# Four layers on one core: an instruction order planned with other delays, single score rounds, sorted waits, and the last layer's output weights multiplied into its key-value sum

## The chip, the core and the metric

The kernel runs on one core of a Trainium2 chip. Its engines work side by side: TensorE (PE; its weight loads stand as PEld), VectorE (DVE), ScalarE (ACT), GpSimd (POOL) and SyncE (SP, here the issuer of all DMAs). The metric is the device time of one execution in microseconds; lower is better. The profile is that of one further execution of the same program.

## The reference

The input x is 2048 rows of 512 columns, in bfloat16. Four layers follow each other, each with a layer norm in front and a residual addition behind. Layers 0 and 2 (called A, same weights) are softmax attention with 32 query heads of size 16 that share one key and one value head. Layers 1 and 3 (called B, same weights) are linear attention with 32 heads.

```python
def _A_ref(x, wq, wk, wv, wo):
    q = (x @ wq).reshape(B, S, H, Dh).transpose(0, 2, 1, 3)
    k, v = x @ wk, x @ wv
    scores = einsum("bhqd,bkd->bhqk", q, k) * (Dh ** -0.5)
    o = einsum("bhqk,bkd->bhqd", softmax(scores), v)
    return o.transpose(0, 2, 1, 3).reshape(B, S, H * Dh) @ wo

def _B_ref(x, wqkv, wo):
    q, k, v = ...
    phi = lambda t: where(t > 0, t + 1, exp(t)) + 1e-6
    pq, pk = phi(q), phi(k)
    kv = einsum("bhsd,bhse->bhde", pk, v)
    z = einsum("bhsd->bhd", pk)
    num = einsum("bhqd,bhde->bhqe", pq, kv)
    den = einsum("bhqd,bhd->bhq", pq, z)[..., None] + 1e-6
    return (num / den).transpose(0, 2, 1, 3).reshape(B, S, D) @ wo

x = x + _A_ref(_layernorm(x), A_wq, A_wk, A_wv, A_wo)
x = x + _B_ref(_layernorm(x), B_wqkv, B_wo)
x = x + _A_ref(_layernorm(x), A_wq, A_wk, A_wv, A_wo)
x = x + _B_ref(_layernorm(x), B_wqkv, B_wo)
```

## The kernel before

**The planner.** The program is not written in its final order. A `Planner` runs a small event simulation while the kernel is built: each operation is created with the engines it may run on, a planned duration, a latency `lat` until its result counts as there, a priority (lower goes first), and the buffers it reads and writes. Python generators (`process`) create operations as flags, buffers (`acq`) and finished operations allow. When an engine is free, `_dispatch1` gives it the ready operation of the lowest priority number, and that order is what is written out, engine by engine. `emit` puts the semaphore waits in front of each instruction: of all operations it depends on, the latest one of each engine, and skips what that engine has waited for already. Each engine then works through its list strictly in order, so an instruction whose input is late holds up all that stand behind it. The planned durations stand as constants (`QK_DUR`, `PV_DUR`, `QK_LAT`, `SWITCH` for a change of the way TensorE's array is divided) or in the calls.

**Layers 0 and 2** (`run_a`). The 2048 rows are 16 tiles of 128. Scores are made in blocks of 128 keys by 512 columns (four heads of a query tile; `j` is one of four row strips of TensorE's array); each layer has 2048 blocks. A score round (L807) issues up to four blocks, one for each row strip. ACT takes two or three blocks of a round at once and writes exponentials (`PT`, L973), out of two sets of three PSUM banks. DVE takes single blocks: it turns a score into the bits of a bfloat16 power of two by one addition and maximum (`FB`, L1049), and after four such blocks makes three shifted copies (L1080), so that each of these blocks is used four times with four weights. A DVE block rides in a round with ACT's blocks, either in the spare bank 7 (`dve_open`, allowed while DVE has under `BLO` us of work queued) or in the third bank of a set (`dve_split`, limits `BLS` and `BLT`). Blocks for DVE are allowed only once the layer's last key tile is there (`KGATE`). The exponentials are multiplied by the values into PSUM bank 6 (L861), four column strips abreast, and DVE collects each segment (L1103, L1105). While TensorE would idle, small matmuls without use are inserted (L906, in other phases L793). Each finished query tile is normalised (L1122 to L1133) and multiplied by `wo` (`epilogue`), and becomes the input of layer 1 or 3.

**Layers 1 and 3** (`run_b`). `tile_` norms a tile and makes its keys and values (`pk`, `va`); `q_` makes its queries: 16 matmuls (L732), then `phi`, which is one Exp on ACT (L1205) and two operations on DVE (L1206, L1208). All this runs, tile by tile, between the exponentials of the layer before. `kv_` sums keys times values over the tiles (L1308), with a column of ones in `va` that gives the key sum; for the last tile it masks the sums into block-diagonal weights `zb` (128x8 a group, L1332) and `kvz` (128x128 a group, L1336). Then, for each tile: `den` multiplies the queries by `zb` (L1358, L1360) and DVE takes reciprocals (L1364); `main` multiplies the queries by `kvz` (L1416), DVE multiplies by the reciprocals (`OB`, L1420), TensorE transposes (L1435), ACT or DVE copies (`OTB`, L569), TensorE multiplies by the output weights `wo2` (L575) and DVE adds the result to x (L1448). In layer 3 a store to DRAM (SP) follows each tile.

The one activation table that the program loads is at its start (L562), with a small Exp.

Of the kernel before, what the change touches and what calls it, by code (L numbers as in the profile page):

```python
# [7 lines left out]
FP32 = mybir.dt.float32  # L8
# [27 lines left out]
class Planner:  # L36
# [3 lines left out]
    def __init__(self, nc):  # L40
        self.nc = nc
        self.now = 0.0
        self.events = []
        self.seq = 0
        self.ready = {e: [] for e in ENGS}
        self.busy = {e: False for e in ENGS}
        self.until = {e: 0.0 for e in ENGS}
        self.order = {e: [] for e in ENGS}
        self.writer = {}
        self.readers = {}  # L50
        self.flags = {}
# [5 lines left out]
        self.port = 0.0  # L57

# [63 lines left out]
    def _dispatch(self, e):  # L122
        self._dispatch1(e)
        if e == PE and not self.busy[e] and self.idle:
            self.due = [t for t in self.due if t > self.now]
            for f in self.idle:
                f()

    def _dispatch1(self, e):
        if self.busy[e]:  # L130
            return
        h = self.ready[e]
        held = []
        while h:
            x = heapq.heappop(h)
            o = x[2]
            if o.eng is not None:
                continue
            dur, fn = o.opts[e]
            if o.port and self.port > self.now:  # L140
                held.append(x)
                continue
            if e == PE and STICK and o.mode != "row" and o.mode != self.mode != "row":
                like = [y for y in h if y[2].eng is None and y[2].mode == self.mode and y[0] <= o.prio + STICK]
                if like:
# [12 lines left out]
            o.eng, o.fn = e, fn  # L158
            self.order[e].append(o)
            self.busy[e] = True  # L160
            self.until[e] = self.now + dur
            if o.cols:
                self.work(o.cols)
            if o.begun:
                self.at(self.now, o.begun)
            self.at(self.now + dur, lambda: self._freed(e, o))
# [4 lines left out]
        if held and not self.busy[e] and e != PE:  # L171
            self.at(self.port, lambda: self._dispatch(e))
# [123 lines left out]
    def emit(self, e, eng):  # L296
        waited = {}
        for o in self.order[e]:
            need = {}
            for d in o.deps:  # L300
                if not d.isdma and d.eng == e and e not in (DV, AC, PO):
                    continue
                k = ("dma", d.slot) if d.isdma else d.eng
                if k not in need or need[k].value < d.value:
                    need[k] = d
            for k, d in need.items():
                if waited.get(k, 0) >= d.value:
                    continue
                waited[k] = d.value
                eng.wait_ge(d.sem, d.value)  # L310
            ins = o.fn(eng)
            if o.sem is not None:
                ins.then_inc(o.sem, 16 if o.isdma else 1)


class Seg:
# [11 lines left out]
    def take(self, js, back=False):  # L328
# [31 lines left out]
BLO = 3.0  # L360
BLT = 4.0
# [6 lines left out]
DENS = {1: [[0], [1], [2], [3], [4], [5], [6], [7], [8, 9], [10, 11], [12, 13], [14, 15]],  # L368
        3: [[0], [1, 2], [3, 4, 5], [6, 7, 8, 9], [10, 11, 12], [13, 14, 15]]}
# [3 lines left out]
RESA = {1: (), 3: ()}  # L373
# [18 lines left out]
def bass_interleave_layers__grouped_kv_mqa__linear_attn_block__prompt_kernel(  # L392
# [42 lines left out]
    eps1 = sb("eps1", [1, H], BF16)  # L435
    warm = sb("warm", [P, 1], FP32)
# [117 lines left out]
    pool_op(lambda e: e.memset(eps1[:], 1e-6), ["eps"], dur=0.1, prio=2.1)  # L554
    pool_op(lambda e: e.memset(mask8[:], 1.0), ["mask8"], dur=0.3, prio=2.3)
# [242 lines left out]
    def run_a(L):  # L798
# [34 lines left out]
        def pv_try():  # L833
# [32 lines left out]
            o = op({PE: (PV_DUR, fn)}, reads=list({x[3] for x in items}) + [("V" if x[5] is None else "VW", x[0]) for x in items], writes=[B_(ACC)], prio=2.0, lat=0.13, mode="col")  # L866
# [46 lines left out]
        def act_stream():  # L913
# [4 lines left out]
            state["on"] = lin["a"] = True  # L918
            while True:
# [53 lines left out]
                ex = op({AC: (0.05 + 0.4267 * n, lambda e, n=n, s_=s_, p_=p_: e.activation(PT[:, p_, 0:n * 512], ps[:, s_ * 512:(s_ + n) * 512], ACTF.Exp, scale=EXPSC, bias=EXPBIAS))},  # L973
                        writes=bk + [("PT", p_)], prio=1.0, lat=0.17)
                ex.begun = lambda n=n: pl.due.append(pl.now + 0.05 + 0.4267 * n + 0.17)
                pl.give_after(sets, s_, [ex] if split is None else [ex, p1])
                pv_post(ex, [(sg, kt, j, PT[:, p_, i * 512:(i + 1) * 512], ("PT", p_)) for i, (sg, kt, j) in enumerate(group)], [n, [], pt_pool, p_])
            state["done"] = True
            pv_kick()
# [64 lines left out]
        def dve_take(extra, own):  # L1044
# [4 lines left out]
            o = op({DV: (0.60, lambda e: e.tensor_scalar(out=dst.bitcast(I16), in0=bank(b), scalar1=VB, scalar2=VLO, op0=ALU.add, op1=ALU.max))},  # L1049
# [7 lines left out]
            return o  # L1057

# [7 lines left out]
        def dve_shifts(blk, f_, hold):  # L1066
# [3 lines left out]
            for w in range(1, NSH):  # L1070
# [8 lines left out]
                en, du = (PO, n / 1165.0 + 0.25) if pool else (DV, n / 3840.0 + 0.066)  # L1079
# [117 lines left out]
    ph_pool = Pool_(range(NPH))  # L1197

    def run_b(L):
# [3 lines left out]
        def phi(b, dst, key, pr, n=D, join=None, after=()):  # L1203
            i = yield ("acq", ph_pool, pr)
            op({AC: (0.07 + n / 1200.0, lambda e: e.activation(phE[:, i, 0:n], bank(b, n), ACTF.Exp))}, reads=[B_(b)], writes=[("phE", i)], prio=min(pr, 0.9))  # L1205
# [22 lines left out]
        def crit_v(t, sl, pr):  # L1228
# [5 lines left out]
            for h in range(2):  # L1234
                src, dst = bank(bs[h], 256).rearrange("p (h d) -> p h d", d=DH), va_v[:, sl, 16 * h:16 * h + 16, 0:DH]
                c = op({AC: (AH_DUR, lambda e, dst=dst, src=src: e.copy(dst, src))}, writes=[B_(bs[h]), ("va", sl)], prio=pr, join=l)
                l = l or c
                pl.give_after(banks, bs[h], [c])
            yield ("ops", pl.ws(("va", sl)))

        def tile_(t):
# [19 lines left out]
            src, dst = bank(b).rearrange("p (h d) -> p h d", d=DH), va_v[:, sl, :, 0:DH]  # L1261
            if t >= CRIT:
# [7 lines left out]
        def q_(t):  # L1270
            pr = base(t) + 0.01 * t + 0.2
            yield ("flag", ("xnT", L, t))
            yield from until(("xnT", t))
            b = yield ("acq", banks, pr)
            mm4(bank(b), lambda g, k: wqkv[:, k, g * P:(g + 1) * P], lambda k: xnT[:, k, t * P:(t + 1) * P], [("xnT", t), "wqkv"], b, pr)
            yield from phi(b, QT[:, t, :], ("QT", t), pr)
            pl.flag(("bq", L, t))

# [175 lines left out]
        for t in range(T):  # L1454
            pl.process(tile_(t))
            pl.process(q_(t))
            pl.process(main(t))
        for ts in DENS[L]:
            pl.process(den(ts))
        for gi, ts in enumerate(KVG):  # L1460
            pl.process(kv_(gi, ts))
# [50 lines left out]
```

## Time and profile before

| what | us |
|---|---|
| median of 3 runs (1555.47, 1555.51, 1560.37) | 1555.51 |
| the profiled execution | 1556.79 |
| its span, first to last instruction | 1555.1 |
| granted TensorE clock, mean over the span | 0.996 |
| first exponential on ACT starts | 13.6 |
| last exponential of layer 0 ends, first of layer 2 starts | 736.2, 759.5 |
| last exponential of layer 2 ends | 1508.0 |
| first denominator of layer 3 starts | 1519.1 |
| last addition of layer 3 ends | 1552.7 |

The times from the third row on are counted from the span's first instruction. Busy times are unions: where two instructions of an engine overlap, the stretch counts once, while the mean of a group is that of single instructions. A line of the groups gives the kernel line, engine, operation, output and inputs with their shapes, the count, busy us and mean ns, then the idle time in front and what ended most of it. A line of the waits says who waited for whom: us in total, times, longest.

### The profile page before, as it was taken

Reading aid. Unit: us, or ns where it says so; the run is one execution under the profiler, and the core shown is the slowest. Engines: PE = TensorE matmul, PEld = TensorE weight load, DVE = VectorE, ACT = ScalarE, POOL = GpSimd, SP = SyncE. Lnnn points to the kernel's source line nnn. Section 1 sums busy time; section 2 is a strip of 40 time slices with the busy share of each in tenths; the row PEclk is TensorE's granted clock in tenths of the full one; section 3 lists DMA queues with packets and bytes.
Section 4 is the critical chain, followed back from the end, with each engine's and each line's share of the span. In section 5 each row is a group of like instructions: output and inputs, shape, how many; then the busy total and the mean of one; then the engine's idle time right before and its main releaser. Section 6 shows DMA issues by size and latency. Waiting matters only on the chain.

```text
span 1555.1 us, 36056 instructions
## 1 busy us (share of the span) xinstructions
PE 1458.7 (94%) x14602; PEld 535.4 (34%) x14713; DVE 1448.3 (93%) x2707; ACT 1476.8 (95%) x1500; POOL 68.8 (4%) x122
## 2 busy tenths in 40 slices
PE   8998999999999999999999989999999999999999
PEld 4322332333333333333644323323333333333345
DVE  7999999999999999998676799999999999999977
ACT  8999999999999999999699999899999999999982
POOL 4000000000000000000111000000000000000000
PEclk9999999999999999999999999999999999999998
DMA  5100010000000000000000000000000000000001
GB/s 132 47 2 1 8 22 5 8 8 5 8 8 8 5 8 5 1 1 1 2 1 1 1 1 15 15 8 8 6 9 5 8 8 8 5 5 2 1 2 55
DMA packets 40435, 17.55 MB, mean 11 GB/s; under 512 B 34128, under 2 KB 39760, under 8 KB 40272
## 3 DMA queue, kind: packets, MB, share of 16 engines
q1 hardware_dynamic: 40272, 15.25, 4.2%
q8 instruction: 118, 1.93, 0.5%
q14 instruction: 45, 0.37, 0.1%
HBM read 5.28 MB, written 2.10 MB: 5 GB/s over the span
## 4 chain that ended last, share of the span: by engine, by line
PE 32%; issue 23%; DVE 23%; ACT 20%; POOL 1%; DMA 0%; SPq 0%; ACTq 0%; POOLq 0%; DVEq 0%
ACT PT L973 19%; DVE FB L1049 11%; PE ps L861 11%; PE ps L807 9%; DVE FB L1080 6%; PE ps L575 4%; PE ps L906 2%; PE ps L732 2%; PE ps L1122 1%; POOL rs L655 1%; DVE st L651 1%; DVE sacc L1103 1%; PE ps L793 1%; ACT phE L1205 1%; DVE xn L658 1%
## 5 line engine op out<-in xcount | busy, mean ns | idle before, releaser
L973 ACT ACTIVATE PT<-ps 128x1024 bf16<-128x1024 f32 (+1 forms) x1361 | 1424.5, 1180 | 19.9 <-PE ps L861 13.4
L1049 DVE TENSOR_SCALAR FB<-ps 128x512 int16<-128x512 f32 x1017 | 675.0, 686 | 23.5 <-PE ps L807 20.7
L807 PE MATMUL ps<-QT,KM 32*128 32x512 bf16 x4096 | 533.4, 384 | 46.8 <-ACT PT L973 27.9
L861 PE MATMUL ps<-FB,VW 128*32 128x512 bf16 x4068 | 530.4, 385 | 19.5 <-ACT PT L973 9.5
L861 PE MATMUL ps<-PT,V 128*32 128x512 bf16 x3079 | 513.0, 386 | 9.7 <-ACT PT L973 5.6
L1080 DVE TENSOR_SCALAR FB<-FB 128x2048 int16<-128x2048 int16 (+1 forms) x765 | 503.0, 683 | 0.9
L807 PEld LDWEIGHTS ps<-QT,KM 32*128 32x128 bf16 x4096 | 139.8, 91 | 445.3 <-ACT PT L973 203.8
L861 PEld LDWEIGHTS ps<-FB,VW 128*32 128x32 bf16 x4068 | 133.4, 94 | 219.5 <-issue 113.0
L861 PEld LDWEIGHTS ps<-PT,V 128*32 128x32 bf16 x3079 | 125.9, 94 | 111.8 <-issue 56.1
L906 PE MATMUL ps<-QT,V 128*32 128x512 bf16 (+6 forms) x568 | 131.0, 315 | 0.9 <-DVE FB L1049 0.9
L655 POOL TENSOR_TENSOR rs<-ve,mhalf 128x1 f32<-128x1 f32 x64 | 51.7, 811 | 1398.9 <-DVE ve L653 1386.0
L575 PE MATMUL ps<-wqkv,xnT 128*128 128x512 bf16 (+1 forms) x211 | 65.1, 368 | 3.9 <-issue 2.9
L906 PEld LDWEIGHTS ps<-QT,V 128*32 128x32 bf16 x568 | 44.1, 95 | 59.6 <-issue 39.3
L1103 DVE COPY sacc<-ps 128x512 f32<-128x512 f32 x64 | 43.8, 684 | 7.8 <-PE ps L861 7.6
L1205 ACT ACTIVATE phE<-ps 128x512 bf16<-128x512 f32 (+1 forms) x66 | 41.3, 625 | 6.6 <-PE ps L732 4.7
L1122 PE MATMUL ps<-identF,sacc 128*128 128x128 f32 x256 | 45.9, 291 | 1.5 <-DVE sacc L1103 0.8
L732 PE MATMUL ps<-xnT,wqkv 128*128 128x128 bf16 x512 | 44.3, 221 | 0.0
L651 DVE BATCH_NORM_STATS2 st<-x_sb 128x6 f32<-128x512 bf16 x60 | 40.8, 683 | 2.6 <-DMA x_sb<-in_A_x_dram 2.3
L1105 DVE TENSOR_TENSOR sacc<-sacc,ps 128x512 f32<-128x512 f32 x56 | 38.2, 682 | 2.4 <-PE ps L861 2.1
L732 PE MATMUL ps<-xnT,wq 128*128 128x128 bf16 x480 | 38.6, 224 | 0.0
L575 PEld LDWEIGHTS ps<-wqkv,xnT 128*128 128x128 bf16 x272 | 21.8, 97 | 44.9 <-issue 34.2
L732 PEld LDWEIGHTS ps<-xnT,wqkv 128*128 128x128 bf16 x512 | 29.1, 98 | 22.8 <-issue 19.4
(115 smaller groups left out, 671.1 us busy)
## 6 DMA issues: line engine op xcount, KB each, us to landing
out_dram<-x_sb SPq DMA_DIRECT2D x16, 128.0 KB, 1.7
x_sb<-in_A_x_dram SPq DMA_DIRECT2D x3, 512.0 KB, 6.1
wqkv<-in_B_wqkv_dram SPq DMA_DIRECT2D x1, 1536.0 KB, 7.5
xnT<-xn SPq DMA_TRANSPOSE x36, 2.4
x_sb<-in_A_x_dram SPq DMA_DIRECT2D x4, 128.0 KB, 2.2
wq<-in_A_wq_dram SPq DMA_DIRECT2D x1, 512.0 KB, 4.2
wo<-in_A_wo_dram SPq DMA_DIRECT2D x1, 512.0 KB, 4.1
wo<-in_B_wo_dram SPq DMA_DIRECT2D x1, 512.0 KB, 8.5
```

Source lines behind the costliest of these rows:

```text
L575: return e.matmul(dst, lhsT=l, rhs=r, start=(k == 0), stop=(k == len(pairs) - 1))
L655: op({PO: (0.55, lambda e: e.tensor_tensor(out=rs[:, t:t + 1], in0=ve[:, t:t + 1], in1=mhalf[:], op=ALU.pow))}, reads=[("ve", t), "mhalf"] ...
L732: ins = e.matmul(dst[:, g * P:(g + 1) * P], lhsT=lhs(g, k), rhs=rhs(k), start=(k == 0), stop=(k == FT - 1))
L807: return e.matmul(bank(b), lhsT=KM[r, sg.par, kt * P:(kt + 1) * P], rhs=QT[r, sg.t, :], start=True, stop=True)
L861: ins = e.matmul(ps[32 * j:32 * j + 32, ACC * 512:(ACC + 1) * 512], lhsT=V[:, kt, :] if w is None else VW[:, kt, w, :], rhs=ap, start=(k = ...
L906: o = op({PE: (n / 2400.0, lambda e: e.matmul(ps[32 * j:32 * j + 32, b * 512:b * 512 + n], lhsT=V0[:], rhs=QT[:, sg.t, 0:n], start=st, sto ...
L973: ex = op({AC: (0.05 + 0.4267 * n, lambda e, n=n, s_=s_, p_=p_: e.activation(PT[:, p_, 0:n * 512], ps[:, s_ * 512:(s_ + n) * 512], ACTF.Ex ...
L1049: o = op({DV: (0.60, lambda e: e.tensor_scalar(out=dst.bitcast(I16), in0=bank(b), scalar1=VB, scalar2=VLO, op0=ALU.add, op1=ALU.max))}, wr ...
L1080: o = op({en: (du, lambda e, w=w, g_=g_: e.tensor_scalar(out=FB[:, g_, 0:n].bitcast(I16), in0=FB[:, f_, 0:n].bitcast(I16), scalar1=float(w ...
L1103: o = op({DV: (0.6, lambda e, src=src: e.tensor_copy(src, bank(ACC)))}, writes=[B_(ACC), key], prio=0.0, lat=0.15)
L1122: o = op({PE: (0.12, lambda e, c=c: e.transpose(ps[:, b * 512 + c * P:b * 512 + (c + 1) * P], src[:, c * P:(c + 1) * P], identF[:]))}, rea ...
L1205: op({AC: (0.07 + n / 1200.0, lambda e: e.activation(phE[:, i, 0:n], bank(b, n), ACTF.Exp))}, reads=[B_(b)], writes=[("phE", i)], prio=min ...
```

## The change

Planner:

- The planned durations and delays get other values: a score becomes usable 0.438 us after its round starts (0.365 before), a value product 0.215 us after its end (0.13), an exponential 0.21 (0.17); a change of array division is counted less the time that TensorE idled in front of it.
- `soon`: while the flag `calm` stands (from the last exponential of a layer to the first of the next), DVE and ACT do not start an operation if one more urgent by 0.3 will be ready before it would end.
- `alone`: when DVE has under `DXB` = 2 us of work queued and a bank is free, a score round with a single block is issued for DVE alone. `BLO` goes from 3 to 5, `BLT` from 4 to 3.
- `emit` sorts an instruction's waits by the planned end of what they wait for.

Layer 1: the queries of tiles 4 to 13 (`QLATE`) are made only after the flag that layer 0's last exponentials are issued. No more than three tiles of queries (`NBQ`) are in work at a time, and `phi`'s Exp keeps its own priority in the calm phases.

Layer 3: `kvt`, `mix`, `den3` and `main3` take the place of `kv_`, `den` and `main`. The transposed sum (values times keys) is masked into block-diagonal `kvT` and multiplied by `wo2` in four matmuls of 512 columns: M, copied to SBUF. The key sum is masked into `Zbd`, 128x128 a group with each head's sum in all 16 columns of the head, so that four matmuls of 128 columns give a tile's denominators in the layout of the transposed queries, 128x512. ACT takes their Ln (with 1e-6 added) and then Exp of the negative, which is the reciprocal; DVE, for tiles 4, 7 and 10 POOL, multiplies the queries by it; four matmuls of 512 columns with M give the output. For tiles 3, 7 and 11 the residual is added by TensorE (a matmul of x with the identity) and ACT copies the result; else DVE adds. The transposes and the copies `OTB` are gone in this layer.

```diff
@@ Planner
+    def soon(self, e, o, dur):
+        if not self.calm or e not in (DV, AC):
+            return 0.0
+        n = self.near[e] = [x for x in self.near[e] if x[0] > self.now and x[2].eng is None]
+        t = [x[0] for x in n if x[1] + 0.3 < o.prio and x[0] + LAG < self.now + dur]
+        return min(t) if t else 0.0
...
+        if e == DV and self.hungry and (not self.ready[DV] or self.backlog(DV) < DXB):
+            self.hungry[0]()
...
+            w = self.soon(e, o, dur)
+            if w:
+                held.append(x)
+                self.at(w, lambda: self._dispatch(e))
+                break
...
-                    dur += SWITCH
+                    dur += max(SWITCH - (self.now - self.until[e]), ROWIN if o.mode == "row" else 0.0)
...
-            for k, d in need.items():
+            for k, d in sorted(need.items(), key=lambda x: x[1].end):
@@ constants
-QK_DUR = 0.225
-PV_DUR = 0.225
-QK_LAT = 0.365
-SWITCH = 0.105
+QK_DUR = 0.22
+PV_DUR = 0.222
+QK_LAT = 0.438
+SWITCH = 0.107
+ROWIN = 0.07
+PV_LAT = 0.215
+EX_LAT = 0.21
+NBQ = 3
+LAG = 0.15
+QLATE = {1: range(4, 14), 3: ()}
+PQ = (4, 7, 10)
+PQD = 0.9
-BLO = 3.0
-BLT = 4.0
+BLO = 5.0
+DXB = 2.0
+BLT = 3.0
-RESA = {1: (), 3: ()}
+RESA = {1: (), 3: (3, 7, 11)}
@@ run_a
+        def alone():
+            if state["done"] or not USE_DVE or ("K", L, KGATE) not in pl.flags or not banks.free or banks.wait or pl.backlog(DV) > DXB:
+                return
+            hit = dve_hit(set())
+            if hit is None:
+                return
+            x = hit + (banks.free.pop(0),)
+            qo = op({PE: (QK_DUR, lambda e: qk_mm(e, x[3], x[0], x[1], x[2]))}, reads=qk_reads(x[0], [x[1]]), writes=[B_(x[3])], prio=0.1, lat=QK_LAT - QK_DUR, mode="row")
+            qo.cols = 128
+            dve_take(x, True)
@@ run_b, q_
+            if t in QLATE[L]:
+                yield ("flag", ("exps", L - 1))
@@ run_b, new
+        def kvt(gi, ts):
...
+                            if i:
+                                ins = e.matmul(ps[:, b * 512 + g:b * 512 + g + 1], lhsT=pk[:, t % 8, g * P:(g + 1) * P], rhs=va[:, t % 8, H * 17 - 1:H * 17],
+                                               start=(not end and t == ts[0]), stop=(t == ts[-1]), skip_group_check=True)
+                            else:
+                                ins = e.matmul(ps[:, b * 512 + g * P:b * 512 + (g + 1) * P], lhsT=va[:, t % 8, g * P:(g + 1) * P], rhs=pk[:, t % 8, g * P:(g + 1) * P],
+                                               start=(not end and t == ts[0]), stop=(t == ts[-1]), skip_group_check=True)
...
+        def mix(g):
+            pr = 1.45 + 0.001 * g
+            b = yield ("acq", banks, pr)
+            mm(bank(b), [(kvT[:, g, :], wo2[:, g, :])], ["kvT", "wo2"], b, pr, 0.216)
+            dst = FB[:, 0, g * 512:(g + 1) * 512]
+            c = flex(lambda e: e.copy(dst, bank(b)), lambda e: e.tensor_copy(dst, bank(b)), 0.48, 0.6, [], [B_(b), ("FB", 0, g), ("M", g)], pr)
...
+        def den3(t):
+            pr = 1.5 + 0.02 * t - 0.01
...
+                for g in range(4):
+                    ins = e.matmul(ps[:, b * 512 + g * P:b * 512 + (g + 1) * P], lhsT=Zbd[:, g, :], rhs=QT[:, t, g * P:(g + 1) * P], start=True, stop=True)
...
+            o = op({AC: (0.5, lambda e: e.activation(rd, bank(b), ACTF.Ln, bias=epsc[:]))}, reads=["epsc"], writes=[B_(b), ("rd", i)], prio=pr, after=af)
+            pl.give_after(banks, b, [o])
+            op({AC: (0.5, lambda e: e.activation(rd, rd, ACTF.Exp, scale=-1.0))}, writes=[("rd", i)], prio=pr)
+            qn = FB[:, 1 + t // 4, t % 4 * 512:t % 4 * 512 + 512]
+            o = op({(PO if t in PQ else DV): (PQD if t in PQ else 0.6, lambda e: e.tensor_tensor(out=qn, in0=rd, in1=QT[:, t, :], op=ALU.mult))}, reads=[("rd", i), ("QT", t)],
+                   writes=[("qn", t)], prio=pr, after=[("FB", 1 + t // 4, t % 4)])
...
+        def main3(t):
+            pr = 1.5 + 0.02 * t
...
+            if t in RESA[L]:
+                mm(bank(b), [(ident[:], x_sb[:, t, :])] + pairs, [("x", t), "ident"] + keys, b, pr, 1.08)
+                o = op({AC: (0.5, lambda e: e.copy(x_sb[:, t, :], bank(b)))}, writes=[B_(b), ("x", t)], prio=pr)
+            else:
+                mm(bank(b), pairs, keys, b, pr, 0.86 + SW[L] / 2)
+                o = op({DV: (0.6, lambda e: e.tensor_tensor(out=x_sb[:, t, :], in0=x_sb[:, t, :], in1=bank(b), op=ALU.add))},
+                       writes=[B_(b), ("x", t)], prio=pr)
```

More of the change, by code (lines that the diff above doesn't have):

```diff
@@ L57, in __init__ @@
         self.port = 0.0
+        self.calm = False
+        self.hungry = []
+        self.near = {e: [] for e in ENGS}
+    def soon(self, e, o, dur):
[4 more added lines that the diff above has]
+        return min(t) if t else 0.0
     def at(self, t, fn):
@@ L165, in _dispatch1 @@
                 self.at(self.now, o.begun)
+            for u in o.users:
+                if isinstance(u, Op) and u.left == 1 and len(u.opts) == 1:
+                    self.near[list(u.opts)[0]].append((self.now + dur + o.name[1], u.prio, u))
             self.at(self.now + dur, lambda: self._freed(e, o))
@@ L170, in _dispatch1 @@
             heapq.heappush(h, x)
-        if held and not self.busy[e] and e != PE:
+        if held and not self.busy[e] and e != PE and self.port > self.now:
             self.at(self.port, lambda: self._dispatch(e))
@@ L918, in act_stream @@
             state["on"] = lin["a"] = True
+            pl.hungry = [alone]
+            pl.calm = False
             while True:
@@ L978, in act_stream @@
             state["done"] = True
+            pl.hungry = []
+            pl.flag(("exps", L))
+            pl.calm = True
             pv_kick()
@@ L1197, in bass_interleave_layers__grouped_kv_mqa__linear_attn_block__prompt_kernel @@
     ph_pool = Pool_(range(NPH))
+    bq_pool = Pool_(range(NBQ))
+    rd_pool = Pool_(range(12))
     def run_b(L):
@@ L1261, in tile_ @@
             src, dst = bank(b).rearrange("p (h d) -> p h d", d=DH), va_v[:, sl, :, 0:DH]
+            if L == 3:
+                src, dst = bank(b), va[:, sl, 0:D]
             if t >= CRIT:
```

111 lines of the change are left out of this document (98 added, 13 removed).

## The prediction

> **What bounds the kernel now.** I read the page's header and busy line first, then the sums of chosen stretches, the waits, the groups, and at last the timeline of the end. Columns of the stretches: stretch in us, its length, then busy us of PE, PEld, DVE, ACT and POOL, granted clock, DMA share, GB/s.
>
> ```profile
> span 1555.1 us, 36056 instructions
> ...
> PE 1458.7 (94%) x14602; PEld 535.4 (34%) x14713; DVE 1448.3 (93%) x2707; ACT 1476.8 (95%) x1500; POOL 68.8 (4%) x122
> ...
> 75.00:735.00 660.00, 621.63 (x6176) 205.94 (x6218) 643.79 (x1156) 653.79 (x654) 16.76 (x15) 1.00 0.03 6
> 735.00:760.00 25.00, 23.86 (x304) 18.36 (x302) 14.04 (x46) 9.83 (x25) 2.05 (x4) 1.00 0.01 1
> 760.00:880.00 120.00, 113.35 (x1124) 49.88 (x1134) 84.56 (x186) 118.91 (x109) 13.57 (x29) 1.00 0.01 2
> 880.00:1506.00 626.00, 588.05 (x5843) 198.79 (x5889) 607.34 (x1095) 613.56 (x615) 16.34 (x15) 1.00 0.04 6
> 1506.00:1519.00 13.00, 12.96 (x154) 9.81 (x151) 6.67 (x21) 5.96 (x12) 0.55 (x1) 1.00 0.01 3
> 1519.00:1533.00 14.00, 13.78 (x136) 9.36 (x135) 9.17 (x17) 2.67 (x5) 0.00 (x0) 0.63 0.06 20
> 1533.00:1553.00 20.00, 18.67 (x157) 11.03 (x158) 17.83 (x30) 4.66 (x9) 0.00 (x0) 1.00 0.25 84
> ```
>
> Two long stretches (layer 0 to 735, layer 2 from 880) are full on ACT and DVE at once: ACT idles 6.2 and 12.4 us there, DVE 16.2 and 18.7. From 736 to 760 runs the chain that joins layer 1 to layer 2, with ACT idle 15.2 of 25 us; up to 880 ACT is full and DVE idles 35.4. The end, 1506 to 1553, leaves ACT idle and runs 14 us at a granted clock of 0.63.
>
> ```profile
> DVE FB L1049 <- PE ps L807: 20.7, 64, 1.0
> ...
> L973 ACT ACTIVATE PT<-ps 128x1024 bf16<-128x1024 f32 (+1 forms) x1361 | 1424.5, 1180 | 19.9 <-PE ps L861 13.4
> L1049 DVE TENSOR_SCALAR FB<-ps 128x512 int16<-128x512 f32 x1017 | 675.0, 686 | 23.5 <-PE ps L807 20.7
> ...
> L1080 DVE TENSOR_SCALAR FB<-FB 128x2048 int16<-128x2048 int16 (+1 forms) x765 | 503.0, 683 | 0.9
> ```
>
> When VectorE starves in the long stretches, it waits for a score round (64 times, 20.7 us). Of the 4096 score blocks ACT takes 3079 at 1424.5/3079 = 0.463 us each, DVE 1017 at (675.0+503.0)/1017 = 1.158. They share one queue of blocks, so a microsecond freed on ACT shortens a full stretch by 1.158/(1.158+0.463) = 0.71 us, one freed on DVE by 0.29.
>
> ```profile
> 0.80 1.28 ACT L562 ACT_TABLE_LOAD   x1 [0.80 <-PEq L1497]
> 2.09 0.20 ACT L562 ACTIVATE warm<-warm 128x1 f32<-128x1 f32 x1
> ...
> 1541.44 1.28 DVE L1420 TENSOR_TENSOR OB<-ps,rdB 128x512 bf16<-128x512 f32 x2
> ...
> 1544.33 1.28 DVE L1420 TENSOR_TENSOR OB<-ps,rdB 128x512 bf16<-128x512 f32 x2
> ```
>
> The last layer's beat at full clock is 1544.33 - 1541.44 = 2.89 us for two tiles. And the program's only table load stands in front of the first Exp, under that instruction's line.
>
> **The change, part by part.**
>
> *Long stretches: delays, lone rounds, wait order.* No instruction of the exponentials is added or dropped; what can be won is the idle above, 18.6 us of ACT and 34.9 of DVE. All of it is worth 18.6 x 0.71 + 34.9 x 0.29 = 23 us. Longer latencies in the plan recover only waits that stem from a wrong order, and a plan with longer latencies is itself longer; the lone rounds address the 20.7 us of DVE above. I take somewhat over half: -13. Bounds: -23, and on the other side 0, as long as PE hides the lone rounds. What hides them: fillers (L906) of 119.1 us in these two stretches, and 76 us in which PE is not busy. A round takes 0.39 us (L807, mean 384 ns). Thirty of them (34.9/1.158) are 12 us, covered; without cover, an exp waits for each. The reordered waits move no work; they are inside this bound.
>
> *Queries of layer 1, tiles 4 to 13, after the exponentials.* Each takes from the first stretch one Exp (L1205, 0.64 us), a small DVE step (L1206, 0.29), one long one (L1208, 0.68) and 16 matmuls (those of L748 took 1.06 us). Ten are 6.4 us of ACT and 9.7 of DVE: 6.4 x 0.71 + 9.7 x 0.29 = 7.4 us. They land on 15.2 idle us of ACT in the chain and the 46 idle us of DVE behind 735; PE gives up its fillers there (L793, 7.4 us) for 10 us of matmuls. No DMA moves; the queue passed is PE's own, where a group of four (0.23 us) can stand in front of the chain about ten times: 2.3 us back. Sum -5; bounds -7.4 and, if all ten Exps slip behind 760 where ACT is full, -7.4 + 4.6 + 2.3 = -0.5.
>
> *Last layer.* Up to the key-value sum the chain stays. The two masks become two of 128x512: the first costs 0.69 (DVE's rate for that shape) in place of 0.27, so +0.4. It removes for 16 tiles the small denominators (1519.12 on, where the clock then falls to 0.50), the product L1420, four transposes L1435 and the copy out. It adds four M products and copies once, and for each tile four 128-column matmuls, a Ln and an Exp on ACT over 128x512, one product (DVE, three on POOL) and four 512-column matmuls. PE: 16 x (0.22 + 0.87) + 0.9 + three residual matmuls 0.6 = 19 us. DVE: 26 x 0.6 = 16. POOL's three have no row; between 0.55 (its shortest, L655) and four times L702's 0.415 = 1.7 us, they lie beside 16 others. Neither is the bound; ACT is: 32 ops at 0.48 (two copies in 1.07 us at 1527.30) to 0.64 are 15.4 to 20.5, I take 17.5, and 5 copies 2.4.
>
> *Table loads.* No row has a Ln. Its price as an operation is bounded by those two figures; the question is whether it runs on the table that is loaded. The load was placed for the instruction behind it, an Exp; nothing in the profile says that a Ln was looked for. If it is another table, each change of function costs one load. By the priorities (1.49 + 0.02t for both, Exp ready 0.08 us after its Ln ends) the plan starts the next tile's Ln in that gap, then two Exps, then two Ln: about nine groups of each, 18 loads, 18 x 1.283 = 23.1 us. Bounds: one load, 1.3 us, and one before each operation, 32 x 1.283 = 41 us. I take 18.
>
> [...]
>
> The end then: first Ln at 1519.1 + 0.4 + 0.4 (its matmuls) = 1519.9; ACT 17.5 + 2.4 + 23.1 = 43.0, to 1562.9; behind it the last product 0.69, matmuls 1.0, addition 0.69 and three hand-overs, 2.7: 1565.6. Before, the last addition ended at 1552.7: +12.9.
>
> **Sum.** 1555.1 - 13 - 5 + 12.9 = 1550.0 of span. That profiled execution took 1556.79 us, 1.7 around its span, and the median of the runs is 1555.51, so 0.4 goes on top: 1550.4, say 1551.
>
> **The rivals.**
>
> *One table holds both.* For it: copies and Exps ran all through on one load; against it, the place of that load. The end is then 1519.9 + 16 + 2.4 + 2.7 = 1541.0, 11.7 earlier than before, without the stretch at half clock: 1555.1 - 18 - 11.7 + 0.4 = 1526. [...]
>
> *A load at every tile (slower).* If a Ln is not ready when the one before ends (banks held by additions, PE late), Ln and Exp take turns: up to 32 loads, 18.0 us more, and no overlap left, 20.5 for 17.5: 1550.4 + 18 + 3 = 1571. It decides from about 25 loads on (7 x 1.283 = 9 us over my sum). For it: denominators, M and outputs share seven PSUM banks; against it: PE needs 0.22 us for a tile that ACT holds for over one.
>
> *Lone rounds swamp PE (slower).* The rule fires whenever DVE has under 2 us queued and a bank is free; blocks that now ride with ACT's rounds may all travel alone. PE has 119 + 76 = 195 us, 500 rounds of 0.39; at 560 it is 23 us short, and the 13 us above are gone: 1586. Against it: score rounds outrank them.
>
> **Chances.** My case 0.55, its own range 1536 to 1566; one table 0.22; a load each tile 0.15; swamped PE 0.08. This kernel's measurement can tell about 0.3% (4.7 us) from no change. Within my case 0.42 lies below 1550.8, 0.30 within, 0.28 above: faster 0.55 x 0.42 + 0.22 = 0.45, same 0.16, slower 0.39. The range takes in most of the one-table case and of the load each tile: 1523 to 1574.
>
> **What would show it.** ACT's table loads between the last exponential and the end: about 18, one, or 32. The span from the last exponential to the last addition: 45 us before; 58 by my sum, 34 with one table. Layer 0's exponentials should end about 14 us earlier than 736.2 (half of the 13, and 7.4), layer 2's 18 earlier than 1508, with DVE's wait for L807 well under 20.7 us and L906's fillers still there; were they gone, PE is swamped. The chain from one to the other (736.2 to 759.5) should grow by no more than 2 us. I am wrong if the exponentials end as late as before, or if ACT is not what the end waits for.

## The result

The changed kernel took 1567.93 us, median of 4 runs (1565.29 to 1568.59), beside 1557.94 for the kernel before on the same chip: a ratio of 1.007, 95% interval 1.0054 to 1.0085. It is slower; 1551 and faster was forecast.

First the head of the page of the changed kernel: its span and the busy line.

```profile
span 1566.0 us, 35820 instructions
...
PE 1452.4 (93%) x14503; PEld 529.9 (34%) x14608; DVE 1451.3 (93%) x2715; ACT 1514.5 (97%) x1523; POOL 66.3 (4%) x126
```

ACT is busy 37.7 us longer in a span that is 10.9 us longer. Next the sums of chosen stretches, with the columns that they had before, cut where layer 0's and layer 2's exponentials end now.

```profile
75.00:730.00 655.00, 615.12 (x6089) 203.06 (x6131) 639.76 (x1145) 649.63 (x627) 13.89 (x15) 1.00 0.03 6
735.00:760.00 25.00, 24.01 (x322) 19.36 (x321) 20.05 (x61) 15.43 (x35) 2.60 (x5) 1.00 0.01 2
...
880.00:1500.00 620.00, 583.93 (x5848) 196.55 (x5890) 603.46 (x1092) 611.88 (x608) 12.90 (x15) 1.00 0.04 7
1500.00:1512.00 12.00, 11.87 (x155) 9.30 (x151) 6.41 (x18) 4.67 (x12) 0.55 (x1) 1.00 0.01 3
1512.00:1540.00 28.00, 16.27 (x113) 8.15 (x113) 12.34 (x19) 27.18 (x34) 2.31 (x2) 0.88 0.10 33
1540.00:1564.00 24.00, 14.63 (x57) 5.59 (x59) 8.52 (x13) 18.44 (x23) 1.15 (x1) 0.73 0.13 44
```

From 1512 on ACT is full (27.18 of 28 us) where it was idle before, and TensorE's granted clock is 0.88 and then 0.73. In the long stretches ACT still idles 5.4 and 8.1 us (6.2 and 12.4 before), DVE 15.2 and 16.5 (16.2 and 18.7): about a quarter of ACT's idle time has gone, and a tenth of DVE's. The groups say the same: ACT's exponentials, then DVE's first step.

```profile
L1005 ACT ACTIVATE PT<-ps 128x1024 bf16<-128x1024 f32 (+1 forms) x1340 | 1421.9, 1176 | 14.8 <-PE ps L891 8.6
L1084 DVE TENSOR_SCALAR FB<-ps 128x512 int16<-128x512 f32 x1030 | 677.6, 684 | 23.3 <-PE ps L837 20.0
```

DVE took 1030 blocks instead of 1017, yet it waits for score rounds (L837, once L807) 20.0 us against 20.7. Last, ACT's timeline in the end, each line a start, a duration and the instructions:

```profile
1523.06 1.28 ACT L1424 ACT_TABLE_LOAD   x1
1524.36 1.26 ACT L1424 ACTIVATE FB<-ps,epsc 128x512 f32<-128x512 f32 x2
1525.64 1.28 ACT L1426 ACT_TABLE_LOAD   x1
1526.93 1.15 ACT L1426 ACTIVATE FB<-FB 128x512 f32<-128x512 f32 x2
1528.10 1.28 ACT L1424 ACT_TABLE_LOAD   x1
```

Two Ln, a load, two Exp, a load: two tiles in 1528.10 - 1523.06 = 5.04 us, against 2.89 before. The trace has 18 such loads, nine for each function, besides the one at the start.

| us from the span's start | before | after | moved by |
|---|---|---|---|
| layer 0's exponentials end | 736.2 | 730.3 | -5.9 |
| layer 2's begin | 759.5 | 755.6 | chain 23.3 to 25.3: +2.0 |
| layer 2's end | 1508.0 | 1500.7 | -7.3 |
| from there to the span's end | 47.1 | 65.3 | +18.2 |
| span | 1555.1 | 1566.0 | +10.9 |

Two things are to be explained: why the end grew by 18.2 and not by 12.9, and why the exponentials end 7.3 us earlier and not 18.

### The profile page after: what moved, and what is told of

It is laid out like the page before. It is cut to its first block, busy times and chain, and to the rows that moved or that the text cites. A ratio compares the mean times of both kernels' runs of the same rounds, so it can differ in the third digit from the quotient of the medians.

```text
span 1566.0 us, 35820 instructions
## 1 busy us (share of the span) xinstructions
PE 1452.4 (93%) x14503; PEld 529.9 (34%) x14608; DVE 1451.3 (93%) x2715; ACT 1514.5 (97%) x1523; POOL 66.3 (4%) x126
## 4 chain that ended last, share of the span: by engine, by line
DVE 39%; PE 36%; ACT 20%; issue 5%; POOL 0%; ACTq 0%; POOLq 0%; DVEq 0%
DVE FB L1084 20%; ACT PT L1005 16%; PE ps L891 14%; DVE FB L1126 12%; PE ps L837 11%; PE ps L605 4%; PE ps L762 2%; PE ps L936 2%; PE ps L1168 2%; DVE sacc L1149 1%; DVE sacc L1151 1%; ACT phE L1253 1%; DVE QT L1256 1%; ACT L1424 1%; ACT L1426 1%
## 5 line engine op out<-in xcount | busy, mean ns | idle before, releaser
L1005 ACT ACTIVATE PT<-ps 128x1024 bf16<-128x1024 f32 (+1 forms) x1340 | 1421.9, 1176 | 14.8 <-PE ps L891 8.6
L1084 DVE TENSOR_SCALAR FB<-ps 128x512 int16<-128x512 f32 x1030 | 677.6, 684 | 23.3 <-PE ps L837 20.0
L837 PE MATMUL ps<-QT,KM 32*128 32x512 bf16 x4096 | 542.0, 384 | 50.6 <-ACT PT L1005 24.6
L891 PE MATMUL ps<-FB,VW 128*32 128x512 bf16 x4120 | 539.3, 384 | 15.5 <-ACT PT L1005 5.7
L1126 DVE TENSOR_SCALAR FB<-FB 128x2048 int16<-128x2048 int16 x777 | 506.3, 678 | 1.0
L837 PEld LDWEIGHTS ps<-QT,KM 32*128 32x128 bf16 x4096 | 141.9, 91 | 452.6 <-ACT PT L1005 158.9
L891 PEld LDWEIGHTS ps<-FB,VW 128*32 128x32 bf16 x4120 | 138.3, 94 | 210.1 <-issue 112.7
L891 PEld LDWEIGHTS ps<-PT,V 128*32 128x32 bf16 x3066 | 127.0, 94 | 111.5 <-issue 63.1
L936 PE MATMUL ps<-QT,V 128*32 128x512 bf16 (+6 forms) x572 | 141.7, 319 | 0.8 <-DVE FB L1084 0.5
L685 POOL TENSOR_TENSOR rs<-ve,mhalf 128x1 f32<-128x1 f32 x64 | 45.7, 715 | 1394.8 <-DVE ve L683 1393.3
L1253 ACT ACTIVATE phE<-ps 128x512 bf16<-128x512 f32 (+1 forms) x66 | 39.8, 605 | 10.7 <-PE ps L762 5.1
L762 PE MATMUL ps<-xnT,wqkv 128*128 128x128 bf16 x512 | 39.6, 220 | 0.0
L762 PEld LDWEIGHTS ps<-xnT,wqkv 128*128 128x128 bf16 x512 | 29.5, 98 | 12.8 <-issue 10.2
```

The costliest lines, as they stand in the source:

```text
L762: ins = e.matmul(dst[:, g * P:(g + 1) * P], lhsT=lhs(g, k), rhs=rhs(k), start=(k == 0), stop=(k == FT - 1))
L837: return e.matmul(bank(b), lhsT=KM[r, sg.par, kt * P:(kt + 1) * P], rhs=QT[r, sg.t, :], start=True, stop=True)
L891: ins = e.matmul(ps[32 * j:32 * j + 32, ACC * 512:(ACC + 1) * 512], lhsT=V[:, kt, :] if w is None else VW[:, kt, w, :], rhs=ap, start=(k = ...
L936: o = op({PE: (n / 2400.0, lambda e: e.matmul(ps[32 * j:32 * j + 32, b * 512:b * 512 + n], lhsT=V0[:], rhs=QT[:, sg.t, 0:n], start=st, sto ...
L1005: ex = op({AC: (0.051 + 0.4267 * n, lambda e, n=n, s_=s_, p_=p_: e.activation(PT[:, p_, 0:n * 512], ps[:, s_ * 512:(s_ + n) * 512], ACTF.E ...
L1084: o = op({DV: (0.602, lambda e: e.tensor_scalar(out=dst.bitcast(I16), in0=bank(b), scalar1=VB, scalar2=VLO, op0=ALU.add, op1=ALU.max))}, w ...
```

## The experiments

Medians stand beside a median of the kernel before on the same chip. Line numbers differ from the changed kernel's by up to three. Small differences need care: t3 and t4 below issue the same work in the same order up to the end of layer 2, and their exponentials ended at 1508.3 and 1513.1 in the executions profiled. All of that arises in one stretch, from 31 to 45 us, where t4's granted clock was 0.51 and t3's 1.00. The columns are those of the stretches above, t4 first:

```profile
31.00:45.00 14.00, 14.00 (x93) 5.48 (x91) 6.98 (x15) 10.47 (x10) 2.25 (x6) 0.51 0.64 209
```

```profile
31.00:45.00 14.00, 13.06 (x144) 5.71 (x142) 11.41 (x22) 14.00 (x15) 2.08 (x6) 1.00 0.61 208
```

From there to the end of layer 2, t4's exponentials lie 4.8 to 5.0 us behind t3's. Where the clock falls differs from one execution to the next, so times are compared below at equal clock (the mean over a run's span) where it changes the reading.

### The end

**t1, the changed kernel with one table.** A table set with both functions is loaded at the start.

```diff
-    op({AC: (1.6, lambda e: e.activation(warm[:], warm[:], ACTF.Exp))}, ...)
+    def warm_up(e):
+        e.preload_act_table_set("natural_log_exp_and_others")
+        return e.activation(warm[:], warm[:], ACTF.Exp)
```

> The changed kernel, with one line more: a table that holds both Exp and Ln is loaded at the start. Theory (the 18 loads are the loss): they and the overlap they break are gone, 18 x 1.283 = 23 us plus some 2; the time from the last exponential to the end of the span falls from 65.3 to about 41 us, the execution from 1568 to about 1543; the exponentials end where they did, near 1500.7. Rival (the Ln and Exp themselves, or the other work of the fold, are the loss, and the loads lie beside them): the end shortens by less than 8 us, the execution stays above 1560.

1541.71 us against 1556.65, 0.9903 [0.9881, 0.9925]. One load is left, the exponentials end at 1500.7 as in the changed kernel, and from there to the span's end it is 38.3 us in place of 65.3. ACT's timeline and the sums of the end:

```profile
1517.60 1.28 ACT L1427 ACTIVATE FB<-ps,epsc 128x512 f32<-128x512 f32 x2
1518.74 1.17 ACT L1429 ACTIVATE FB<-FB 128x512 f32<-128x512 f32 x2
1519.78 1.29 ACT L1427 ACTIVATE FB<-ps,epsc 128x512 f32<-128x512 f32 x2
```

```profile
1512.00:1526.00 14.00, 13.77 (x117) 7.74 (x115) 11.68 (x19) 13.36 (x25) 2.32 (x2) 1.00 0.17 56
1526.00:1537.00 11.00, 9.97 (x58) 4.40 (x56) 8.42 (x14) 7.49 (x14) 1.16 (x1) 1.00 0.33 109
```

Two tiles now take 1519.78 - 1517.60 = 2.18 us, PE is full and its clock stays at 1.00. By these two executions the 18 loads cost 27.0 us, 1.50 each, though a load lasts 1.283. For what is above that the trace shows two sources, which were not priced apart: a load starts 1.295 before what follows, while two operations in a row overlap (an Ln lasts 0.687 and the next starts 0.586 after it began), and the clock is slower (0.88 and 0.73 against 1.00). Where the set with both is loaded first, Ln and Exp take turns on that one load; the kernel as written has 19 loads in all.

**t2, the changed kernel with the old last layer; t3, the kernel before with the new one (called the fold, since `wo2` is folded into M); t4, t3 with one table.**

```diff
# t2, against after
-            pl.process((main3 if L == 3 else main)(t))
+            pl.process(main(t))
-            pl.process((kvt if L == 3 else kv_)(gi, ts))
+            pl.process(kv_(gi, ts))
...
# t3, against before: the same lines the other way round; t4: t3 with the preload of t1
```

> The changed kernel with layer 3 done as before (no fold); all else of the change stays. Theory (the end is where the change loses, the long stretches win 7 us): the end takes 47 us again, as before the change, instead of 65.3; the execution is near 1550. Rival (the long stretches won nothing on their own, the earlier end of the exponentials in the changed kernel comes from the fold, which leaves the queues emptier there): the exponentials end near 1508 and the execution is at 1555 to 1558.

> The kernel before with the fold of layer 3 alone: old delays, no lone rounds, old waits, queries of layer 1 where they were. Theory: the fold with its 18 or so loads costs what it costs in the changed kernel, 65 us of end against 47, so about 1574. Rival (the loss at the end comes from the other parts, say the calm phase holding operations back): the fold alone is at 1557 or below.

> The kernel before with the fold alone and one table for Exp and Ln. Theory: the end is some 41 us against 47 before, so 6 us faster than the kernel before, about 1551, and 23 to 25 us below the same kernel with 18 loads. Rival (a DVE or PE bound appears in place of the loads): less than 15 us below it, no faster than the kernel before.

| kernel | median | ratio to before | loads | last exponential to span's end |
|---|---|---|---|---|
| t2 | 1551.29 | 0.9965 [0.9951, 0.9979] | 1 | 45.3 |
| t3 | 1575.89 | 1.0123 [1.0097, 1.0148] | 19 | 63.5 |
| t4 | 1551.68 | 0.9961 [0.9946, 0.9977] | 1 | 38.3 |

The folded end costs 16.4 us with the loads on the kernel before (63.5 - 47.1) and 20.0 on the rest of the change (65.3 - 45.3); with one table it saves 8.8 and 7.0. About half of the 8.8 is the clock: r0 below has the old end too, at a clock of 1.00 where before had 0.89, and takes 42.7 us from the last exponential, 4.4 more than t4 at 1.00. All the rest of the change together (t2) is worth 5.4 us.

### The long stretches, one part at a time

Each of these four is the kernel before with one part of the change.

```diff
# s1: moved queries and calm phases
+NBQ = 3
+QLATE = {1: range(4, 14), 3: ()}
+            pl.calm = True
...
# s2: planned delays
-QK_LAT = 0.365
+QK_LAT = 0.438
...
-                    dur += SWITCH
+                    dur += max(SWITCH - (self.now - self.until[e]), ROWIN if o.mode == "row" else 0.0)
# s3: lone rounds
-BLO = 3.0
-BLT = 4.0
+BLO = 5.0
+BLT = 3.0
+            pl.hungry = [alone]
...
# s4: sorted waits
-            for k, d in need.items():
+            for k, d in sorted(need.items(), key=lambda x: x[1].end):
```

> The kernel before with layer 1's queries of tiles 4 to 13 moved behind layer 0's exponentials and the calm rule; nothing else of the change. Theory (the forecast's -5 holds: ten Exps and their DVE work leave the full stretch, the chain behind grows by 2 us): layer 0's exponentials end 6 to 8 us earlier than 736, the chain to layer 2's first is 25 us, the execution 4 to 6 us below before. Rival (what leaves the full stretch is not turned into exponentials, since the plan's order has waits of its own there): layer 0's exponentials end less than 3 us earlier and the execution is at before's time or above.

> The kernel before with the new planned durations and delays alone. Theory (the long stretches won less than forecast because longer planned delays make the planner leave rounds with no block for DVE and start exponentials later; the order is no better for it): the execution is 5 us or more above before, with fewer DVE blocks than 1017 and more exponentials on ACT. Rival (the forecast's reason: true delays give an order with fewer waits): 3 to 10 us below before, idle of ACT and DVE in the two stretches below 18.6 and 34.9 us.

> The kernel before with lone score rounds for DVE (and the limits that go with them) alone. Theory: with the old delays DVE is seldom found hungry in the plan, so some tens of lone rounds, 1 to 5 us below before. Rival 1 (lone rounds are what spoils the long stretches): above before by 3 us or more. Rival 2 (they are the whole win of the long stretches): 7 us or more below.

> The kernel before with sorted waits alone; the order of every engine is that of before. Theory (they move no work): within 2 us of before. Rival (the wait that stands last is the one that the instruction itself carries, so a late wait in front of it costs a dispatch each time; with some 1200 extra waits on ACT and 900 on PE that adds up): 4 us or more below before, the exponentials end earlier in both long stretches.

| kernel | median (before: 1556.44) | ratio | exponentials of layer 0 and 2 end |
|---|---|---|---|
| s1 queries | 1554.91 | 0.9988 [0.9972, 1.0003] | 729.8, 1505.2 |
| s2 delays | 1567.31 | 1.0069 [1.0045, 1.0093] | 745.9, 1519.4 |
| s3 lone rounds | 1552.83 | 0.9987 [0.9970, 1.0004] | 737.1, 1508.0 |
| s4 waits | 1564.28 | 1.0042 [1.0025, 1.0058] | 739.4, 1515.2 |

s1 ends layer 0's exponentials 6.4 us earlier, as expected, but layer 2's only 2.8, and its time differs by too little to be sure of, where 4 to 6 us less were expected. s3's interval takes in 1 as well, but its runs part by the clock: seven at 0.995 to 0.997 took 1550.88 to 1553.27 us, three at 0.988 to 0.991 took 1558.04 to 1561.89, and none of the kernel before at 0.995 to 0.997 beside them was under 1555.30. So at equal clock lone rounds alone read as a win of some 4 us; whether they lower the clock was not tried. Its profile was taken at 0.991 (0.66 from 785 to 800 us), so its 1508.0 is late. s2 loses: at a clock of 0.995 its three runs took 3 to 8 us more than the one of before there (1560.68). The waits of DVE of that kernel say where.

```profile
DVE FB L1082 <- PE ps L836: 32.3, 78, 1.7
```

That is 32.3 us of waiting for score rounds, 20.7 before: with the longer delays alone the plan starves DVE. My further expectation, fewer blocks for DVE and more for ACT, missed: DVE took 1023 against 1017.

s4 was the surprise. By the traces ACT, DVE and POOL issue the same operations in the same order as before, and PE the same but for a few records that start together or are missing; only the order in which an operation's waits are written differs, and it lost 7.8 us. I had expected no difference beyond 2 us, and the rival a gain.

### The order of the waits

What the order changes is seen in the instructions. In the traces, of several waits of one operation, the one written first is carried by the operation itself, and not the one written last, as s4's rival had it; on PE the weight loads carry them (2426 waits in the trace of before, none on a matmul). Each later one is a semaphore instruction of its own ahead of the operation. ACT's stream has 1177 such instructions in all three orders; what differs is which wait they hold. Sorted by planned end, the wait that ends last stands in them.

| ACT's waits on PE | before | s4 | after | r0 |
|---|---|---|---|---|
| in an instruction of its own | 350 | 1169 | 1178 | 7 |
| carried by the operation | 1136 | 317 | 289 | 1479 |

**r0, the kernel before with its waits sorted the other way.**

```diff
+            for k, d in sorted(need.items(), key=lambda x: -x[1].end):
```

> The kernel before with the waits of each instruction sorted the other way round, latest planned end first; no order of an engine changes. Theory (the trace of the sorted-waits kernel shows that the wait written first is the one that the instruction carries, and the later ones stand in front of it as instructions of their own; sorting by end puts the late wait there 1169 times on ACT, against 350 in the kernel before): now the late wait is carried nearly always, so 2 to 5 us below before and 10 to 13 us below the kernel with the waits sorted by end. Rival (what cost 8 us there is chance, or has to do with something else than which wait is carried): within 2 us of before, or above it.

1551.45 us against 1556.55, 0.9969 [0.9957, 0.9981], exponentials to 1503.5. From s4 to r0 nothing but this sign changed, and it is worth 12.8 us, some 12 at equal clock (1560.01 against 1547.87 and 1548.01 at 1.00). In both profiles the clock stays at 1.00 up to the last exponential. The exponentials' group in s4, then in r0:

```profile
L1004 ACT ACTIVATE PT<-ps 128x1024 bf16<-128x1024 f32 (+1 forms) x1361 | 1427.8, 1176 | 23.0 <-PE ps L890 15.5
```

```profile
L1004 ACT ACTIVATE PT<-ps 128x1024 bf16<-128x1024 f32 (+1 forms) x1361 | 1422.8, 1190 | 18.4 <-PE ps L890 13.0
```

In r0 one exponential lasts longer (1190 ns against 1176), yet together they keep ACT busy 5.0 us less, since more of each lies under the one before: 1361 x 14 ns is 19 us more in sum and 5 less in union. Why more of each lies there is not shown. Where ACT idled between two exponentials, the traces of before and after show a difference: the second starts 22 to 24 ns after PE's semaphore update if it carries the wait on PE (54 times), and 81 to 84 ns after it if that wait stands ahead (96 of 98). The idle time in front falls by 4.6 us. That is 9.6 of the 11.7 us by which the exponentials end earlier. On PE the waits of the score rounds' weight loads change too, s4 and then r0:

```profile
PEld ps L836 <- ACT PT L1004: 154.6, 410, 1.0
...
PEld ps L836 <- DVE FB L1082: 67.6, 160, 1.0
```

```profile
PEld ps L836 <- ACT PT L1004: 327.6, 869, 1.0
...
PEld ps L836 <- DVE FB L1082: 49.3, 136, 0.9
```

869 loads in place of 410 have ACT as what ends their wait. In all, the choice of the wait that stands ahead is worth the 12.8 us between s4 and r0. What inside the engine makes it so was not tried.

**b1, the changed kernel with one table and this order; r1, the changed kernel with this order alone.**

```diff
# both
-            for k, d in sorted(need.items(), key=lambda x: x[1].end):
+            for k, d in sorted(need.items(), key=lambda x: -x[1].end):
# b1 also: the preload of t1
```

> The changed kernel with one table for Exp and Ln and the waits sorted latest first. Theory (sorted waits cost the changed kernel what they cost the kernel before, some 8 to 11 us): 1530 to 1534, against 1541.7 with one table alone. Rival (with the changed delays in the plan the waits are met with slack, and which one is carried no longer matters): 1539 or more.

> The changed kernel with its waits sorted latest first, and nothing else: the 18 table loads stay. Theory (the two losses stand side by side and add: loads some 26 us, sorted waits 11): 1555 to 1559, level with the kernel before, exponentials ending near 1490 and an end of 63 to 65 us. Rival (with the loads in the end, ACT's order there makes the waits count for less, or the waits cost only in the end): 1563 or more.

b1 took 1530.65 us against 1556.55, 0.9838 [0.9821, 0.9855]: the fastest kernel here, 11.1 below t1. r1 took 1556.22 against 1555.53, 0.9998 [0.9985, 1.0011], 11.7 below the changed kernel's median; its 19 loads are still there and its end takes 63.1 us. Its exponentials end at 1489.1, 18.9 earlier than before. So the two losses add up: the order of the waits some 11 us, the loads some 26 (r1 to b1: 25.6). b1's head and the groups that answer to those above:

```profile
span 1527.1 us, 35907 instructions
...
PE 1460.9 (96%) x14608; PEld 521.0 (34%) x14608; DVE 1444.1 (95%) x2715; ACT 1482.9 (97%) x1505; POOL 67.6 (4%) x126
...
L1008 ACT ACTIVATE PT<-ps 128x1024 bf16<-128x1024 f32 (+1 forms) x1340 | 1415.8, 1186 | 11.4 <-PE ps L894 6.4
L1087 DVE TENSOR_SCALAR FB<-ps 128x512 int16<-128x512 f32 x1030 | 673.0, 680 | 19.5 <-PE ps L840 18.0
```

Against the changed kernel, the exponentials' busy time falls from 1421.9 to 1415.8 and the idle time in front of them from 14.8 to 11.4.

### The parts beside one another

Since s2 had lost alone, b2 takes the new delays out of b1, b3 the lone rounds as well, d1 the lone rounds only, and q0 the moved queries with the calm phases.

```diff
# b2, against b1
-QK_LAT = 0.438
+QK_LAT = 0.365
...
# d1, against b1; b3 is both
-            pl.hungry = [alone]
+            pl.hungry = []
...
# q0, against b1
-QLATE = {1: range(4, 14), 3: ()}
+QLATE = {1: (), 3: ()}
...
```

> As the one before (one table, waits latest first), but with the planned durations and delays of the kernel before. Theory (the new delays cost, as they did alone, +11 us): 5 to 11 us below the one before, 1521 to 1527. Rival (the delays cost only without lone rounds, which fill the holes that they leave in the plan; together they are at least neutral): the same as the one before or slower.

> As the one before (one table, waits latest first, old delays), but without lone rounds and with the old limits. Theory (lone rounds win a few us by keeping DVE fed): 2 to 6 us above the one before. Rival (they only shift work to PE): no more than 1 us above, or below.

> One table, waits latest first, new delays, but no lone rounds and the old limits: the fourth corner beside 1530.7 (delays and lone rounds), 1538.1 (lone rounds, old delays) and 1542.6 (neither). Theory (new delays alone leave DVE without blocks, as in the kernel with the delays alone, and lone rounds fill just that): above 1546, with fewer DVE blocks than 1020. Rival (the two are worth 7.5 and 4.5 us independently): near 1535.

> As the fastest so far (one table, waits latest first, new delays, lone rounds), but layer 1's queries where they were and no calm phases. Theory (moving them is worth the 5 us of the forecast, where alone it showed 1.5): 1534 to 1538. Rival (it is worth no more than alone): 1530 to 1533.

| median, us (ratio to before) | with lone rounds | without |
|---|---|---|
| new delays | b1 1530.65 (0.9838) | d1 1547.35 (0.9950 [0.9931, 0.9968]) |
| old delays | b2 1538.12 (0.9885 [0.9867, 0.9903]) | b3 1542.62 (0.9915 [0.9900, 0.9930]) |

My theory for b2, faster than b1, fell; the rival held. The two parts need each other: the new delays win 7.5 us beside lone rounds and lose 4.7 without them, and lone rounds win 16.7 with the new delays, 4.5 with the old. DVE's waits in d1 and in b1 show the one that is mended:

```profile
DVE FB L1087 <- PE ps L840: 28.1, 79, 1.2
```

```profile
DVE FB L1087 <- PE ps L840: 18.0, 46, 2.3
```

d1's plan has 2 rounds of a single block and 136 of four, b1's 71 and 68. Why the longer delays alone make the plan starve DVE was not separated further; that d1's DVE would get under 1020 blocks missed (1026), as in s2.

q0 took 1541.77 us, 0.9906 [0.9889, 0.9924]: without the moved queries and the calm phases 11.1 us are lost beside the other parts, more than theory or rival had, though alone they brought no clear gain in s1. Why they are worth more in company was not tried.

## Why the prediction was wrong

**The step that failed** is the sentence "The reordered waits move no work; they are inside this bound." They moved no work, but they cost time: alone +7.8 us (s4), and the opposite order wins 11 to 12 in the changed kernel (r1, b1). The term for the waits was put at nothing because I looked for idle time that the plan could win back, and not at what an instruction looks like once its waits are written. The order could have been weighed from the trace of before, which has 350 of ACT's waits on PE in instructions of their own and 1136 carried, but not priced from it.

**Long stretches, forecast -13 and -5, measured -7.3 at the last exponential.** The kernel before in its three orders ended the exponentials at 1515.2, 1508.0 and 1503.5. An estimate from these: with its waits unsorted the changed kernel would have ended them at 1500.7 - 7.2, and by r1 at 1489.1 + 4.5, both near 1493.5, 14.5 earlier than before; the two agree because the whole step between the sorted orders is the same in both kernels (11.7 and 11.6). So the waits took 7.2 of the 10.7 us that the forecast lacked, and some 3.5 were too much hope. How the gain is split among the parts was also misjudged: moved queries with the calm phases are worth 11 us beside the others, not 5, and the delays win nothing without the lone rounds. Layer 0's exponentials ended 5.9 us earlier, not 14. That DVE's wait would fall "well under 20.7 us" was wrong; it was 20.0. The bounds of the two terms, -23 to 0 and -7.4 to -0.5, still hold what was measured; it is their middle that was 10.7 us off.

**The chain between the layers** grew by 2.0 us; "no more than 2" and the term 2.3 held.

**The end, forecast +12.9, measured +18.2.** The mechanism was right to the count: 18 loads, nine groups of each function, and ACT is what the end waits for (DVE's product, L1428, idles 59.5 us in all for it). The size was off in three places. The first load starts 12.4 us after the last exponential, where the first Ln was put 11.9 after it: 0.5. From that load to the last Exp's end ACT takes 45.5 us (1513.1 to 1558.6), not 43.0: the 18 loads 18 x 1.295 = 23.3, operations and copies 22.2 in place of 19.9. From there to the last addition's end it is 5.0 us (to 1563.67), not 2.7, since two tiles' matmuls queue behind the last Exps at a clock of 0.73. Together 5.3.

**The rivals.** One table was not what the kernel got, but as a mechanism it was priced to 3.0 us: t1's end of 38.3 us ends the additions at 1536.7 where the forecast's terms, moved to exponentials that end at 1500.7, give 1541.0 - 7.3 = 1533.7. A load at each tile did not come: both functions went for the most part in pairs. Lone rounds did not swamp PE: 71 single-block rounds of 1410, and the fillers are as many as before (572 against 568).

**The sum.** 10.7 us from the exponentials and 5.3 from the end make 16.0, which is the 1566.0 of span against the forecast 1550.0. Without the first the span would be 1555.3, level with before; without the second 1560.7, 5.6 above it. So the exponentials' share made the change slower and not level, and the forecast's win needed both. The waits' 7.2 alone leave 1558.8, 3.7 above before, within the 4.7 that the prediction calls no change; r1, with the better order, came out level too. The stated range, 1523 to 1574, holds the measured time, but it took in most of two rivals; my case's own, 1536 to 1566, does not, and the direction was wrong.

## What to carry to other kernels

Two functions of ACT that alternate are to be counted in loads (here 18 of 1.283 us, for Ln and Exp); where one set holds both, try loading it before the first use: here one line took 27 us off the end. Of several waits, write the one that will end last first, so that the operation carries it; some 12 us lay between the two orders of otherwise equal streams. Parts of a planner's change are to be tried beside one another: here the delays lost alone and won 7.5 us in company. Before two profiles are compared, look at where the granted clock fell in each.

## What was not expected of the hardware

- ACT's exponentials take less time together when they carry the wait that ends last (r0) than when it stands in a semaphore instruction ahead (s4): 1422.8 us of union against 1427.8 for the same 1361, and 18.4 us of idle time in front against 23.0.
- The granted clock fell to 0.88 and 0.73 where PE was busy for 16.27 of 28 and 14.63 of 24 us, between the loads. From the last exponential on it was 0.84 in the changed kernel, 0.89 in t3 and 0.83 in r1, all with the loads, and 1.00 in t1, t4 and b1, with one table. PE's busy share alone does not set it: before, it was 0.63 in a stretch with PE busy for 13.78 of 14 us. What does was not tried.
- The clock fell in one execution and not in another over the same work: 0.51 in t4 and 1.00 in t3 from 31 to 45 us, and 0.89 in s4 and 1.00 in r0 over the old end.
- POOL's product of 128x512 took 1.153 us, between the 0.55 and 1.7 that bounded it; ACT's Ln 0.687, above the 0.64 that did.
